# Routed experts after attention: the first two expert tiles share their split weights, VectorE subtracts for all tiles

## The chip, the cores and the metric

One core of a Trainium2 chip runs the whole program in one launch. The metric is the device time of one execution in microseconds (us), lower is better. The engines are called as in the profile: PE (TensorE matmul), PEld (its weight loads), DVE (VectorE), ACT (ScalarE), POOL (GpSimd), SP (SyncE, which issues most transfers).

## What is computed

```python
def reference(**kwargs):
    attn_out = _attn_ref(**attn_kwargs)          # sigmoid attention, 4 x 12 heads x 448 x 64
    x = np.ascontiguousarray(attn_out.transpose(0, 2, 1, 3)).reshape(B * S, H * D)
    x = _moe_ref(x=x, **moe_kwargs)              # 8 experts, one per token
    return _moe2_ref(x=x, **moe2_kwargs)         # sigmoid(x @ w_gate) * (x @ w_val) @ w_out

def _moe_ref(x, expert_emb, tau, w1, w2):        # x 1792 x 768, w1 8 x 768 x 1024, w2 8 x 1024 x 768
    ...
    expert_idx = np.argmax(logits, axis=1)
    ...
    for e in range(E):
        mask = expert_idx == e
        h = np.maximum(x[mask] @ w1[e], 0.0)
        out[mask] = gate_w[mask, None] * (h @ w2[e])
```

Everything is float32. The kernel keeps nearly that precision by writing each float32 operand as a high and a low part in the type fp32r and adding three products: high times high, low times high, high times low.

## The kernel before

The program runs three parts in a row. **Attention** works through 24 pairs of heads. **The experts** follow: tokens are sorted by expert into tiles of 128 rows; `NSTAT` = 14 tiles are written out in the program, further ones sit behind run-time branches (`tail_tiles`, L1074). **The feed-forward part** comes last.

For an expert tile p, `gather` (L791) fetches its 128 rows of x by an indirect transfer that POOL issues; `front` (L798) turns them by PE transposes, and ACT and DVE write the parts xh and xl; `h_chunk` (L923) multiplies by w1 in four chunks c of 9 matmuls; ACT applies relu; `turn` (L949) turns h and writes its parts (hh, hl, for tile 0 w64, w32); `y_chunk` (L965) multiplies by w2 in four chunks of 12 matmuls; `y_scale` and `y_out` weight the rows and scatter them.

Weights come as chunks of 128 x 1536. The list `order` (L128) names the chunks in the sequence in which they are used, `load` (L162) issues a chunk's transfer into one of eight raw buffers, `split_next` (L216) makes the next chunk's parts, and `take` hands them to the product. A split is a cast on ACT (hi) and a subtraction lo = raw - hi (L213), on DVE or, where `split_next` is given `G`, on POOL. The parts live in a ring of `RING` = 4 buffers: a cast for a chunk waits until the product of the chunk four places earlier is done.

Tiles 0 and 1 belong to the same expert, the fullest one, so that tile 1 needs no transfer; its w1 chunks are split a second time from the same raw buffers (`order` lists w1 for p = 0 and p = 1).

Between attention and tile 2 stands the routing: some 90 small DVE steps on tables of 128 x 8 to 128 x 208. `place_a` (L587) counts tiles per expert, `place_b` (L633) makes the table of experts, `place_c` (L673) the rows' places `am`; POOL multiplies them by row numbers (spi, L559), PE sums (psid, `ids_all`, L684), and DVE casts the sums into idx, the row numbers that `gather` of tiles 2 and on needs. `gate_a` to `gate_d` (L727 to L759) make the rows' weights: a root on POOL, a normalisation on DVE, an exponential on ACT, three multiplications on POOL (spg, L559), sums on PE (psg), and gate_s, which `y_scale` needs. PE's stream holds psid and psg between products, so it stands still if they are late.

No scheduler decides the order: the program's text, with `manual_schedule`, is the order on each engine, and each engine runs its own instructions strictly in that order. The four PSUM buffers (`slot`) are shared by all products.

```python
    G0 = 2 * NPR * (B - 1) + 2
    for g in range(2 * NP + 1):                                  # L834, attention
        ...
        if g == 2 * NP:
            split_next(eng=G, hi_eng=V)                          # L847, w1 chunk 3
    ...
    h_chunk(0, 0, lambda: count(TE, NT))                         # L1175
    ...
    for c in range(NW1):                                         # L1206, tile 1
        h_chunk(1, c)
        split_next(ahead, V if c in (0, 3) else G)
```

Of the kernel before, what the change touches and what calls it, by code (L numbers as in the profile page):

```python
# [105 lines left out]
def routed_kernel(ctx: ExitStack, tc: tile.TileContext, kqP, vP, emb, tau, w1P, w2P, wffP, cst, out):  # L106
# [21 lines left out]
    order = [("w1", p, c) for p in range(2) for c in range(NW1)] + [("w2", 0, c) for c in range(NW2)]  # L128
# [33 lines left out]
    def load(i):  # L162
        it, r = order[i], raws[raw_of[i]]
        if it[0] in ("w1", "w2"):
            w, (_, p, c) = {"w1": w1P, "w2": w2P}[it[0]], it

            if p != 1:
                e = expert_of(p)
                src = w[bass.ds(e, 1), :, c * CH : (c + 1) * CH].rearrange("a p f -> p (a f)")
                SP.dma_start(r, src, cond=(e != expert_of(p - 1)) if p else None)  # L170
# [38 lines left out]
    def split(raw, pool, name, width=CH, eng=V, hi_eng=None):  # L209
        hi = pool.tile([P, width], F32R, tag="hi", name=f"hi{name}")[:, : raw.shape[1]]  # L210
        lo = pool.tile([P, width], F32R, tag="lo", name=f"lo{name}")[:, : raw.shape[1]]
        (hi_eng.tensor_copy if hi_eng else A.copy)(hi, raw)  # L212
        eng.tensor_sub(lo, raw, hi)  # L213
        return hi, lo

    def split_next(ahead=None, eng=V, hi_eng=None):  # L216
# [4 lines left out]
        parts[i] = split(raws[raw_of[i]], ring, i, eng=eng, hi_eng=hi_eng)  # L221
# [610 lines left out]

    G0 = 2 * NPR * (B - 1) + 2
    for g in range(2 * NP + 1):  # L834
# [11 lines left out]
        if g == 2 * NP:  # L846
            split_next(eng=G, hi_eng=V)  # L847
# [63 lines left out]
        if q in (6, 7, 8):  # L911
            split_next(hi_eng=V if q == 7 else None)
# [10 lines left out]
    def h_chunk(p, c, between=None):  # L923
# [4 lines left out]
        hi, lo = take()  # L928
# [246 lines left out]
    h_chunk(0, 0, lambda: count(TE, NT))  # L1175
# [8 lines left out]
    h_chunk(0, 1, lambda: first_ids(1, NT))  # L1184
# [8 lines left out]
    place_a()  # L1193
    for k in range(2, NW2):
        load(order.index(("w2", 0, k)))
    ahead = []
    split_next(ahead)
    split_next(ahead, G)
    h_chunk(0, 2)
    split_next(ahead, G)  # L1200
    h_chunk(0, 3)
    front(1)
    turn(0, dp, ("w64", "w32"))
    gate_a()
    split_next(ahead)
    for c in range(NW1):  # L1206
        h_chunk(1, c)
        split_next(ahead, V if c in (0, 3) else G)
        if c == 0:
            place_b()  # L1210
    for i in ahead:
        load(i)

    part = [take() for _ in range(NW2)]
    y_chunk(0, 0, part[0])
    turn(1)
    place_c()
    gate_b()
    gate_exp()
    for c in range(1, NW2):  # L1220
        y_chunk(0, c, part[c])
    for c in range(NW2):
        y_chunk(1, c, part[c])
        if c == 0:
            ids_all()
            gather(2)
            gate_c()
            gather(3)
        if c == 2:
# [8 lines left out]
    for p in range(2, NSTAT):  # L1238
# [5 lines left out]
        for c in range(NW1):  # L1244
# [7 lines left out]
            split_next(None, G if p == 2 and c in (1, 3) else V)  # L1252
# [159 lines left out]
```

## Time and profile before

| | before |
|---|---|
| median of 3 runs | 1037.21 us (1036.66 to 1038.28) |
| profiled execution | 1037.45 us, span 1035.6 us |
| PE busy, share of the span | 1006.4 us, 97% |
| DVE busy | 597.2 us, 58% |
| ACT busy | 503.1 us, 49% |
| POOL busy | 138.4 us, 13% |

A row of the timeline gives the start of an instruction in us from the span's start, its duration, engine, line, operation, outputs and inputs with their shapes, how many equal ones are merged (x), and in brackets how long the engine was idle before it and what ended that. Such a duration includes time in which an instruction that has begun is held up. The view of waits sums the idle time by who ended it. A window gives, for a stretch of time, each engine's busy time and the clock that TensorE was granted as a share of full speed (1.00 is 2.4 GHz, 0.50 is 1.2 GHz).

### The profile page before, as it was taken

The numbers are of one execution on the slowest core, as the hardware profiler recorded it, in microseconds if no ns is written. First come the engines' busy times: TensorE is split into PE (matmuls) and PEld (weight loads), VectorE is DVE, ScalarE is ACT, GpSimd is POOL, SyncE is SP. The second block draws the span as 40 slices with busy tenths as digits, with TensorE's granted clock in tenths as the row PEclk, the third lists the DMA queues.
The fourth block names the chain that finished last, engine by engine and source line by source line (L and its number), as shares of the span: only waits on it lengthen the run. The fifth ranks groups of instructions, "written<-read, shape, count | busy, mean of one in ns | idle before, by whom it ended". The sixth has DMA issues, their size and how long they took to land.

```text
span 1035.6 us, 15304 instructions
## 1 busy us (share of the span) xinstructions
PE 1006.4 (97%) x6144; PEld 822.7 (79%) x6144; DVE 597.2 (58%) x660; ACT 503.1 (49%) x546; POOL 138.4 (13%) x109
## 2 busy tenths in 40 slices
PE   9999999878999999999999999999999999999996
PEld 4455455676887788888888899888899888899995
DVE  5665577986887877787658743334332333323551
ACT  5576678536766676777502432233322333323540
POOL 0010012643242122111100000200000000001001
PEclk9999999989999999999999999999999999999998
DMA  7878786112689876765458652422333333324630
GB/s 254 303 257 300 247 304 231 71 32 110 247 265 415 289 263 269 253 221 211 166 169 280 236 180 99 143 99 92 122 122 123 125 108 103 122 92 143 196 119 31
DMA packets 38526, 191.94 MB, mean 185 GB/s; under 512 B 4952, under 2 KB 5992, under 8 KB 36016
## 3 DMA queue, kind: packets, MB, share of 16 engines
q1 hardware_dynamic: 30560, 152.84, 43.3%
q0 software_dynamic: 7888, 38.05, 9.8%
q8 instruction: 50, 0.82, 0.3%
q14 instruction: 28, 0.23, 0.1%
HBM read 197.46 MB, written 31.16 MB: 221 GB/s over the span
## 4 chain that ended last, share of the span: by engine, by line
PE 73%; DVE 0%; issue 0%; DMA 0%; POOLq 0%; ACT 0%
PE gv L1154 11%; PE gv L1153 11%; PE gv L1155 11%; PE h L935 8%; PE o L921 5%; PE o L919 5%; PE o L920 5%; PE y L919 3%; PE y L921 3%; PE y L920 3%; PE qh L1024 1%; PE qy L1047 1%; PE hTp L954 1%; PE yTp L1139 1%; PE xTp L803 1%
## 5 line engine op out<-in xcount | busy, mean ns | idle before, releaser
L213 DVE TENSOR_TENSOR lo<-rawb,hi 128x1536 fp32r<-128x1536 f32 x173 | 302.1, 1756 | 289.9 <-ACT hi L212 286.3
L212 ACT CAST hi<-rawb 128x1536 fp32r<-128x1536 f32 x178 | 262.8, 1480 | 244.7 <-PE gv L1154 96.3
L1153 PE MATMUL gv<-yT,hi 128*128 128x512 f32 (+1 forms) x576 | 208.9, 363 | 0.0
L1155 PE MATMUL gv<-yT,lo 128*128 128x512 f32 (+1 forms) x576 | 208.9, 363 | 0.0
L1154 PE MATMUL gv<-yT,hi 128*128 128x512 f32 (+1 forms) x576 | 208.8, 363 | 0.0
L1155 PEld LDWEIGHTS gv<-yT,lo 128*128 128x128 f32 x576 | 108.7, 189 | 16.9
L1153 PEld LDWEIGHTS gv<-yT,hi 128*128 128x128 f32 x576 | 108.7, 189 | 16.8
L1154 PEld LDWEIGHTS gv<-yT,hi 128*128 128x128 f32 x576 | 108.7, 189 | 16.7
L919 PE MATMUL o<-hi,gh 128*128 128x384 f32 x336 | 112.8, 336 | 0.0
L921 PE MATMUL o<-lo,gh 128*128 128x384 f32 x336 | 112.3, 334 | 0.0
L920 PE MATMUL o<-hi,gl 128*128 128x384 f32 x336 | 112.3, 334 | 0.0
L359 ACT ACTIVATE attn<-sc,bias_s 112x896 f32<-112x896 f32 x96 | 91.2, 1001 | 41.9 <-PE sc L358 41.9
L1324 ACT CAST gh<-sg 128x512 fp32r<-128x512 f32 (+1 forms) x48 | 27.2, 567 | 132.1 <-DVE sg L1323 132.1
L364 PE MATMUL av<-attn,v 112*64 112x448 f32 x384 | 82.8, 552 | 0.0
L919 PE MATMUL y<-hi,hh 128*128 128x384 f32 x208 | 72.7, 349 | 0.0
L935 PE MATMUL h<-hi,xh 128*128 128x512 f32 x168 | 69.2, 412 | 3.5 <-PEq L1078 3.4
L935 PE MATMUL h<-lo,xh 128*128 128x512 f32 x168 | 67.1, 399 | 4.5 <-DVE lo L213 4.5
L921 PE MATMUL y<-lo,hh 128*128 128x384 f32 x208 | 70.5, 339 | 0.3 <-DVE lo L213 0.3
L920 PE MATMUL y<-hi,hl 128*128 128x384 f32 x208 | 70.3, 338 | 0.0
L1343 POOL DMA_INDIRECT out<-ob,idc x13 | 17.8, 1373 | 370.5 <-DVE ob L1372 340.1
L920 PEld LDWEIGHTS o<-hi,gl 128*128 128x128 f32 x336 | 63.1, 188 | 0.1
L919 PEld LDWEIGHTS o<-hi,gh 128*128 128x128 f32 x336 | 63.1, 188 | 0.1
(302 smaller groups left out, 1311.9 us busy)
## 6 DMA issues: line engine op xcount, KB each, us to landing
rawb<-wd SPq DMA_DIRECT2D x65, 768.0 KB
rawb<-in_w1P SPq DMA_DIRECT2D x52, 768.0 KB
rawb<-in_w2P SPq DMA_DIRECT2D x52, 768.0 KB
rawb<-in_wffP SPq DMA_DIRECT2D x16, 1536.0 KB
wd<-rawb POOLq DMA_DIRECT2D x16, 768.0 KB, 7.9
kq<-in_kqP SPq DMA_DIRECT2D x24, 448.0 KB
v<-in_vP SPq DMA_DIRECT2D x24, 224.0 KB
xd<-xr_sb POOLq DMA_DIRECT2D x12, 336.0 KB, 5.2
```

What stands on the lines that cost most here:

```text
L212: (hi_eng.tensor_copy if hi_eng else A.copy)(hi, raw)
L213: eng.tensor_sub(lo, raw, hi)
L359: A.activation(at_, ps[:CP, :, :S], AF.Sigmoid, bias=bias_s[:CP], scale=1.0 / math.sqrt(HD))
L364: T.matmul(pav_t[i][j * HD : (j + 1) * HD, 0, :S], v[:, c, j * HD : (j + 1) * HD], attn_t[i, c][:, j, :], start=(c == 0), stop=(c == NCH - 1))
L919: T.matmul(o, ah[:, ks], bh[:, w], start=(k == 0), stop=False)
L920: T.matmul(o, al[:, ks], bh[:, w], start=False, stop=False)
L921: T.matmul(o, ah[:, ks], bl[:, w], start=False, stop=(k == nk - 1))
L935: T.matmul(ps[:, half, :], x[:, k * P : (k + 1) * P], w[:, s * 512 : (s + 1) * 512], start=(k == 0 and x is xh and w is hi), stop=(k == KD ...
L1153: T.matmul(o, hi[:, a, k, :], yh[:, k, :n], start=(k == 0), stop=False)
L1154: T.matmul(o, hi[:, a, k, :], yl[:, k, :n], start=False, stop=False)
L1155: T.matmul(o, lo[:, a, k, :], yh[:, k, :n], start=False, stop=(k == KD - 1))
L1324: A.copy(gh[:, f, :n], sg[:, :n])
```

## The change

- `order` lists w1 for tile 0 alone. `h_chunk` takes a chunk's parts as an argument, and `w1_0` holds the four chunks' parts until tile 1 has used them too. Four splits go: of twelve for tiles 0 and 1 there remain eight.
- `split` and `split_next` lose their engine argument: DVE does every subtraction. The cast of w1 chunk 3, which DVE made at the end of attention (L847), is made by ACT behind `first_ids` of tile 1.
- The steps between tile 0's w1 product and tile 2 stand in another order: `place_a` and `gate_a` behind tile 0's w1 product, then `front(1)`, `place_b`, the transfers `ahead`, `place_c`, and only then `turn(0)`, tile 1's w1 product with the splits of w2, `ids_all` and the gathers of tiles 2 and 3, before tile 0's first w2 chunk; `gate_b`, `gate_exp` before `turn(1)`; `gate_c` before tile 1's w2 product; `front(2)`, `gate_d` and `y_scale(0)` behind its second chunk, not its third.

```diff
--- before.py
+++ after.py
@@ -125,7 +125,8 @@
 
     rawb = rawp.tile([P, RAWS, CH], F32, name="rawb")
     raws = [rawb[:, i, :] for i in range(RAWS)]
-    order = [("w1", p, c) for p in range(2) for c in range(NW1)] + [("w2", 0, c) for c in range(NW2)]
+
+    order = [("w1", 0, c) for c in range(NW1)] + [("w2", 0, c) for c in range(NW2)]
     order += [("w1", 2, c) for c in range(NW1)]
     for p in range(3, NSTAT):
         order += [("w1", p, c) for c in range(NW1)]
@@ -163,11 +164,9 @@
         it, r = order[i], raws[raw_of[i]]
         if it[0] in ("w1", "w2"):
             w, (_, p, c) = {"w1": w1P, "w2": w2P}[it[0]], it
-
-            if p != 1:
-                e = expert_of(p)
-                src = w[bass.ds(e, 1), :, c * CH : (c + 1) * CH].rearrange("a p f -> p (a f)")
-                SP.dma_start(r, src, cond=(e != expert_of(p - 1)) if p else None)
+            e = expert_of(p)
+            src = w[bass.ds(e, 1), :, c * CH : (c + 1) * CH].rearrange("a p f -> p (a f)")
+            SP.dma_start(r, src, cond=(e != expert_of(p - 1)) if p else None)
         elif it[0] == "gv":
             if it[1] == 0 and it[2] in direct:
                 if it[2] - 2 not in direct:
@@ -206,19 +205,19 @@
     parts = {}
     done_split = [0]
 
-    def split(raw, pool, name, width=CH, eng=V, hi_eng=None):
+    def split(raw, pool, name, width=CH, hi_eng=None):
         hi = pool.tile([P, width], F32R, tag="hi", name=f"hi{name}")[:, : raw.shape[1]]
         lo = pool.tile([P, width], F32R, tag="lo", name=f"lo{name}")[:, : raw.shape[1]]
         (hi_eng.tensor_copy if hi_eng else A.copy)(hi, raw)
-        eng.tensor_sub(lo, raw, hi)
+        V.tensor_sub(lo, raw, hi)
         return hi, lo
 
-    def split_next(ahead=None, eng=V, hi_eng=None):
+    def split_next(ahead=None, hi_eng=None):
         i = done_split[0]
         if i >= len(order):
             return
         done_split[0] += 1
-        parts[i] = split(raws[raw_of[i]], ring, i, eng=eng, hi_eng=hi_eng)
+        parts[i] = split(raws[raw_of[i]], ring, i, hi_eng=hi_eng)
         j = next((j for j in range(i + 1, len(order)) if order[j][:2] == ("gv", 0) and order[j][2] in direct), None)
         if j == i + 1:
             f = order[j][2]
@@ -830,6 +829,8 @@
         split_pair(n)
         load_pair(n + 3)
 
+    ahead = []
+
     G0 = 2 * NPR * (B - 1) + 2
     for g in range(2 * NP + 1):
         i, hh = divmod(g, 2)
@@ -843,8 +844,6 @@
         elif g == 4:
             prepare_experts()
         q = g - G0
-        if g == 2 * NP:
-            split_next(eng=G, hi_eng=V)
         ia, ha = divmod(g - 1, 2)
         if q == 2:
             count(0, TE)
@@ -909,7 +908,7 @@
             for k in (0, 1):
                 load(order.index(("w2", 0, k)))
         if q in (6, 7, 8):
-            split_next(hi_eng=V if q == 7 else None)
+            split_next(ahead, hi_eng=V if q == 7 else None)
 
     hp_t = {}
 
@@ -920,12 +919,12 @@
         T.matmul(o, al[:, ks], bh[:, w], start=False, stop=False)
         T.matmul(o, ah[:, ks], bl[:, w], start=False, stop=(k == nk - 1))
 
-    def h_chunk(p, c, between=None):
+    def h_chunk(p, c, between=None, part=None):
         if c == 0:
             hp_t[p] = slot(f"h{p}")
         ps = hp_t[p]
         xh, xl = xg_t["T", p]
-        hi, lo = take()
+        hi, lo = part or take()
 
         passes = ((xh, hi), (xh, lo), (xl, hi))
         for part in (passes[:2], passes[2:]) if c == 0 else (passes,):
@@ -1172,7 +1171,8 @@
     A.copy(x.rearrange("p (b c) n -> p b c n", c=2), pv[:, :, :, :P])
     SP.dma_start(xd[TE * CP :, D - P :].rearrange("(c p) n -> p c n", p=CP), x)
     choose(TE, NT)
-    h_chunk(0, 0, lambda: count(TE, NT))
+    w1_0 = [take() for _ in range(NW1 - 1)]
+    h_chunk(0, 0, lambda: count(TE, NT), part=w1_0[0])
     fullest_ids(TE, NT)
     for f in squares:
         f()
@@ -1181,7 +1181,7 @@
     ranks(TE, NT)
     first_tiles(TE, NT, (1,))
     columns(TE, NT)
-    h_chunk(0, 1, lambda: first_ids(1, NT))
+    h_chunk(0, 1, lambda: first_ids(1, NT), part=w1_0[1])
     at.close()
     yTp = ctx.enter_context(tc.tile_pool(name="yT", bufs=1, reuse_waits="tile"))
     ytp = ctx.enter_context(tc.tile_pool(name="yt", bufs=2, reuse_waits="tile"))
@@ -1190,43 +1190,38 @@
     decp = ExitStack()
     dp = decp.enter_context(tc.tile_pool(name="dec", bufs=1, side="right", reuse_waits="tile"))
     gather(1)
-    place_a()
     for k in range(2, NW2):
         load(order.index(("w2", 0, k)))
-    ahead = []
     split_next(ahead)
-    split_next(ahead, G)
-    h_chunk(0, 2)
-    split_next(ahead, G)
-    h_chunk(0, 3)
+    w1_0.append(take())
+    h_chunk(0, 2, part=w1_0[2])
+    h_chunk(0, 3, part=w1_0[3])
+    place_a()
+    gate_a()
     front(1)
-    turn(0, dp, ("w64", "w32"))
-    gate_a()
-    split_next(ahead)
-    for c in range(NW1):
-        h_chunk(1, c)
-        split_next(ahead, V if c in (0, 3) else G)
-        if c == 0:
-            place_b()
+    place_b()
     for i in ahead:
         load(i)
+    place_c()
+    turn(0, dp, ("w64", "w32"))
+    for c in range(NW1):
+        h_chunk(1, c, part=w1_0[c])
+        split_next()
+    ids_all()
+    gather(2)
+    gather(3)
 
     part = [take() for _ in range(NW2)]
     y_chunk(0, 0, part[0])
-    turn(1)
-    place_c()
     gate_b()
     gate_exp()
+    turn(1)
     for c in range(1, NW2):
         y_chunk(0, c, part[c])
+    gate_c()
     for c in range(NW2):
         y_chunk(1, c, part[c])
-        if c == 0:
-            ids_all()
-            gather(2)
-            gate_c()
-            gather(3)
-        if c == 2:
+        if c == 1:
             front(2)
             gate_d()
             y_scale(0)
@@ -1249,7 +1244,7 @@
                 turn(2)
                 small_ids()
                 gather_small()
-            split_next(None, G if p == 2 and c in (1, 3) else V)
+            split_next()
             if c == 1 and p - PZ in (0, 1, 3):
                 small_step((0, 2, 0, 6)[p - PZ])
             if dec and c % 2 == 0:
```

The line numbers of the changed kernel are one to five lower. In the names below, the number behind lo, hi is the chunk's place in `order`: before, 0 to 3 are w1 for tile 0, 4 to 7 for tile 1, 8 to 11 w2 of both, 12 to 19 w1 of tiles 2 and 3; in the change, 0 to 3 are w1 of both tiles, 4 to 7 w2, 8 to 15 w1 of tiles 2 and 3.

POOL, from the end of attention to the gather of tile 4. Before:

```order
L213 TENSOR_TENSOR lo3_1995<-rawb_91,hi3_1994 128x1536
L794 DMA xg1_2126<-xd_71,idx01_139 128x768
L213 TENSOR_TENSOR lo5_2170<-rawb_91,hi5_2169 128x1536
L213 TENSOR_TENSOR lo6_2183<-rawb_91,hi6_2182 128x1536
L730 TENSOR_TENSOR root_158<-ss_118,half_s_109 112x16
L213 TENSOR_TENSOR lo9_2289<-rawb_91,hi9_2288 128x1536
L213 TENSOR_TENSOR lo10_2302<-rawb_91,hi10_2301 128x1536
L559 TENSOR_TENSOR spi_2371<-am_151,ids_h_113 112x416
L794 DMA xg2_2450<-xd_71,idx_133 128x768
L559 TENSOR_TENSOR spg_2462<-am_151,g3_2456 112x16x26 x3
L794 DMA xg3_2466<-xd_71,idx_133 128x768
L794 DMA xg4_2569<-xd_71,idx_133 128x768
```

In the change:

```order
L793 DMA xg1_2122<-xd_71,idx01_139 128x768
L729 TENSOR_TENSOR root_158<-ss_118,half_s_109 112x16
L558 TENSOR_TENSOR spi_2257<-am_151,ids_h_113 112x416
L793 DMA xg2_2350<-xd_71,idx_133 128x768
L793 DMA xg3_2352<-xd_71,idx_133 128x768
L558 TENSOR_TENSOR spg_2435<-am_151,g3_2429 112x16x26 x3
L793 DMA xg4_2553<-xd_71,idx_133 128x768
```

The five subtractions are gone from POOL, as are two more behind the gather of tile 4 (lo17, lo19); the root, spi and spg remain in the same order, and the gather of tile 3 stands ahead of spg.

DVE, the end of `place_a` (offs is its last result) up to the first step of `place_b` (end). Before:

```order
L619 TENSOR_TENSOR offs_145<-offs_145,nz_2152 128x8
L213 TENSOR_TENSOR lo4_2166<-rawb_91,hi4_2165 128x1536
L809 TENSOR_TENSOR xl1_2206<-xTp1_2198,xh1_2205 128x768
L960 TENSOR_TENSOR w320_2219<-hTp0_2209,w640_2218 128x1024
L729 TENSOR_REDUCE ss_118<-ssp_119 112x4
L731 TENSOR_TENSOR sh_159<-lg_117,mx_120 112x128
L213 TENSOR_TENSOR lo7_2226<-rawb_91,hi7_2225 128x1536
L213 TENSOR_TENSOR lo8_2240<-rawb_91,hi8_2239 128x1536
L636 TENSOR_TENSOR end_2243<-offs_145,st_144 128x8
```

In the change:

```order
L618 TENSOR_TENSOR offs_145<-offs_145,nz_2175 128x8
L728 TENSOR_REDUCE ss_118<-ssp_119 112x4
L730 TENSOR_TENSOR sh_159<-lg_117,mx_120 112x128
L808 TENSOR_TENSOR xl1_2197<-xTp1_2189,xh1_2196 128x768
L635 TENSOR_TENSOR end_2200<-offs_145,st_144 128x8
```

Four subtractions, of weights and of h, that stood between `place_a` and `place_b` are gone from there or stand later.

DVE, from the last step of `place_c` (am) to the first of `gate_b` (root). Before, with the two subtractions ahead of `place_c`:

```order
L670 CAST et_2277<-ef_2274 1x26
L213 TENSOR_TENSOR lo11_2317<-rawb_91,hi11_2316 128x1536
L960 TENSOR_TENSOR hl1_2360<-hTp1_2350,hh1_2359 128x1024
L675 CAST ky_2363<-tn_156 128x26
L676 TENSOR_TENSOR s3_131<-oh_123,cs_92 112x128
L678 TENSOR_REDUCE po_2366<-s3_131 112x16
L680 TENSOR_TENSOR ab_2368<-ai_140,po_2366 112x16
L681 TENSOR_TENSOR am_151<-ky_2363,ab_2368 112x416
L299 TENSOR_SCALAR root_158<-root_158 112x16
```

In the change:

```order
L680 TENSOR_TENSOR am_151<-ky_2249,ab_2254 112x416
L959 TENSOR_TENSOR w320_2269<-hTp0_2259,w640_2268 128x1024
L212 TENSOR_TENSOR lo4_2283<-rawb_91,hi4_2282 128x1536
L212 TENSOR_TENSOR lo5_2297<-rawb_91,hi5_2296 128x1536
L212 TENSOR_TENSOR lo6_2311<-rawb_91,hi6_2310 128x1536
L212 TENSOR_TENSOR lo7_2327<-rawb_91,hi7_2326 128x1536
L685 CAST idx_133<-psid_2331 128x26
L686 COPY idf_154<-psid_2331 32x5
L298 TENSOR_SCALAR root_158<-root_158 112x16
```

Tile 0's h (w32) and the four w2 subtractions now stand in one row behind `place_c`, and idx ahead of the normalisation. The subtraction hl of tile 1 stands seven rows further down, behind the normalisation.

## Rows read from the trace of the kernel before

**Rows 1.** Waits of PE, whole span (engine line waited for: us in total, times, longest us).
```profile
PE y L921 <- DVE lo L213: 4.0, 2, 3.7
```

**Rows 2.** Two windows of 10 us: busy of PE, PEld, DVE, ACT, POOL, granted clock, DMA.
```profile
230.00:240.00 10.00, 10.00 (x52) 8.85 (x50) 5.91 (x7) 7.37 (x6) 1.92 (x3) 0.87 0.41 116
...
240.00:250.00 10.00, 6.55 (x26) 4.98 (x25) 7.07 (x7) 4.47 (x4) 6.62 (x2) 0.83 0.31 126
```

**Rows 3.** Timeline of POOL, 185 to 230 us (start us, us, engine line op, names, shapes).
```profile
185.01 6.88 POOL L213 TENSOR_TENSOR lo<-rawb,hi 128x1536 fp32r<-128x1536 f32 x2 [1.59 <-ACT hi L212]
...
196.94 4.60 POOL L730 TENSOR_TENSOR root<-ss,half_s 112x16 f32<-112x16 f32 x1 [5.05 <-DVE ss L729]
...
202.23 6.96 POOL L213 TENSOR_TENSOR lo<-rawb,hi 128x1536 fp32r<-128x1536 f32 x2 [0.68 <-ACT hi L212]
...
225.43 3.99 POOL L559 TENSOR_TENSOR spg<-am,g 112x416 f16<-112x416 f16 x1
```

**Rows 4.** Timeline of DVE: the long steps, and one of usual length.
```profile
185.17 3.35 DVE L610 TENSOR_TENSOR st<-st,qz 128x8 f32<-128x8 f32 x1
...
188.56 3.37 DVE L613 COPY ns<-st 128x8 f32<-128x8 f32 x1
...
192.10 0.17 DVE L616 TENSOR_TENSOR ns<-tot,nz 128x8 f32<-128x8 f32 x1
...
202.38 3.40 DVE L647 TENSOR_TENSOR isa<-cs,nq 128x26 f32<-128x26 f32 x1
...
205.70 3.54 DVE L648 TENSOR_TENSOR jbv<-cs,nq 128x26 f32<-128x26 f32 x1
```

**Rows 5.** Timeline of ACT, 180 to 221 us.
```profile
180.91 1.46 ACT L212 CAST hi<-rawb 128x1536 fp32r<-128x1536 f32 x1
...
189.01 0.81 ACT L808 CAST xh<-xTp 128x768 fp32r<-128x768 f32 x1 [0.40 <-PE xTp L803]
...
207.66 1.02 ACT L959 CAST hh<-hTp 128x1024 fp32r<-128x1024 f32 x1 [0.50 <-PE hTp L954]
...
220.47 0.31 ACT L738 ACTIVATE sh<-sh 112x128 f32<-112x128 f32 x1 [10.49 <-DVE sh L735]
```

**Rows 6.** Timeline of DVE: where each routing step begins.
```profile
182.03 0.15 DVE L589 COPY tot<-pk 128x8 f32<-128x8 f32 x1
...
193.05 1.75 DVE L213 TENSOR_TENSOR lo<-rawb,hi 128x1536 fp32r<-128x1536 f32 x1
...
201.67 0.16 DVE L636 TENSOR_TENSOR end<-offs,st 128x8 f32<-128x8 f32 x1
...
214.08 1.76 DVE L213 TENSOR_TENSOR lo<-rawb,hi 128x1536 fp32r<-128x1536 f32 x1
...
216.89 0.17 DVE L675 CAST ky<-tn 128x26 f16<-128x26 f32 x1
...
218.32 0.17 DVE L299 TENSOR_SCALAR root<-root 112x16 f32<-112x16 f32 x1
...
222.01 0.26 DVE L742 TENSOR_REDUCE gs<-sh 112x16 f32<-112x128 f32 x1
...
225.27 3.41 DVE L213 TENSOR_TENSOR lo<-rawb,hi 128x1536 fp32r<-128x1536 f32 x2
```

**Rows 7.** Chain that ended last, one whole h product of a later tile.
```profile
292.19 8.20 PE h L935 x36
```

**Rows 8.** Timeline of PE, 194 to 234 us.
```profile
194.85 0.60 PE L935 MATMUL h<-lo,xh 128*128 128x512 f32 x1 [4.49 <-DVE lo L213]
...
204.50 0.34 PE L919 MATMUL y<-hi,w 128*128 128x384 f32 x1
...
206.59 1.03 PE L954 MATMUL hTp<-cs,hr 128*128 128x128 f32 x8
...
229.47 1.20 PE L566 MATMUL psg<-spg,bm 112*128 112x78 f16 x16 [2.35 <-POOL spg L559]
...
233.66 0.39 PE L935 MATMUL h<-hi,xh 128*128 128x512 f32 x1
```

## The prediction

> **What bounds the kernel now.** The page of the profile comes first: PE is busy for 97% of the span, DVE for 58%, POOL for 13%. Elsewhere PE is the limit, and only what PE loses can be won. PE's timeline and the view of its waits say where. Before 194.85 PE stood still for 4.49 us, in tile 1's w1 product, for a DVE subtraction lo [rows 8]. The w2 products waited 4.0 us for such a lo, in two waits of which the longer took 3.7 us [rows 1]. Before psg, at 229.47, PE waited 2.35 us for POOL's spg [rows 8]. All this is the stretch that the change rewrites. After such waits the granted clock of a 10 us window is below 1 (0.87 and 0.83 [rows 2]): half clock for a while, so that each wait costs more than itself.
>
> Why is DVE late there? In its timeline, four table steps of 128 x 8 or 128 x 26 take 3.35, 3.37, 3.40 and 3.54 us; one of the same 128 x 8 shape takes 0.17 [rows 4]. POOL's timeline explains it. POOL runs two subtractions back to back from 185.01 for 6.88 us, to 191.89; the two long steps begin at 185.17 and 188.56, and the second ends at 191.93. Again POOL from 202.23 for 6.96 us, to 209.19, and the other two long steps fill 202.38 to 209.24 [rows 3, 4]. While POOL subtracts, DVE gets one small step through per subtraction. So a subtraction given to POOL does not relieve DVE: it takes about 3.4 us of DVE's time, where DVE's own takes 1.75 [rows 6].
>
> The Trainium skill states the mechanism (SBUF — State Buffer, Who interferes with whom): a DVE instruction with two SBUF inputs, or in a two-port mode, and a GpSimd instruction that reads SBUF exclude each other for a whole instruction, whichever began first. The trace agrees, with the four steps above. Another page speaks against the change (Perfetto Trace Analysis, Optimizing Scalar/DVE Operations): where DVE is saturated, moving work off it to GpSimd may pay, though it warns that the two share a port. By that rule alone, DVE, which in the new order is busy almost without a break from 191 to 208 us, would only become later; by the rows it gets 3.4 us back for each 1.75 us taken over. The sum below uses the rows alone.
>
> **The change, part by part.** I follow the new order on the old trace's clock. Durations are differences of starts.
>
> *DVE.* ACT casts w1 chunk 3 at 180.91 and is done at 182.4 [rows 5], before PE needs that chunk. The subtraction takes 1.75: 184.1. `place_a` took 182.03 to 193.05, 11.02 us, of which the two long steps are 6.72; at 0.17 each it takes 4.6: 188.8. `gate_a` has two steps: 189.1. xl1 waits for xh1, which ACT ends at 189.82 [rows 5], then takes some 1.0: 190.8. `place_b` took 201.67 to 214.08, 12.4 us, with 6.94 in long steps, hence 5.8: 196.6. `place_c` 216.89 to 218.32, 1.4: 198.1. Tile 0's h: one subtraction of weights and one of h took 214.08 to 216.89, so the latter 1.1: 199.2. The four w2 subtractions at 1.7 (two take 3.41): 206.0. The casts of idx, 0.2, and the normalisation, 218.32 to the exponential at 220.47, 2.15: 208.4. Then ACT's exponential 0.31 and its cast of tile 1's h 1.02 with two handovers: 209.8; hl 1.1 to 1.2: 211.0. `gate_c`, 222.01 to 225.27, 3.3: 214.2 [all rows 6, 5].
>
> *POOL.* The root took 4.60 us; it can start at 189 and is wanted at 206. spi follows `place_c`. spg's third part took 3.99 us in the old order, because two DVE subtractions began just ahead of it at 225.27 and held it up for 3.41 us [rows 3, 6]: it ended 0.74 us after them, which I take as what it needs. Now at most one subtraction can go ahead of it (lo8, whose cast waits for tile 1's first w2 chunk). spg is ready at 215.0, or at 216.8 if lo8 wins.
>
> *PE.* xh1 is there at 189.8, the parts of w1 are those of tile 0, xl1 comes at 190.8 while six matmuls run: no wait. The product takes 8.2 us [rows 7]: 198.1, where it used to end at 204.50 [rows 8]. This is the first stall with its slow stretch. Then psid waits about 1 us for spi, and tile 0's w2 product for lo4 at 199.2 + 1.7 = 200.9; psid's small matmuls lie inside that. A w2 chunk takes 2.09 us (204.50 to 206.59 [rows 8]). Ten of the first twelve matmuls, the turn of tile 1 (1.0) and three chunks: 209.9; lo5 to lo7 are always there in time. Tile 1's second matmul waits for hl, 211.0; two chunks: 215.0; front(2), six transposes against the turn's eight in 1.03 us, 0.8: 215.8; psg at 215.8 or 216.8, 0.6 (1.20 at half clock [rows 8]); two chunks: tile 2 begins at 220.6 to 221.6. Before it began at 233.66 [rows 8]. **Gain 12.1 to 13.1 us.** Behind that, ACT waits for gate_s before it casts w1 chunks 1 to 3 of tile 2: lo8 and xl2 end at 218, gate_s at 219, ACT's scaling (0.9) and cast (1.46) at 221.4, lo9 at 223.1; its use stands at 222.9, so 0.2 us is lost.
>
> *Tile 2.* Two subtractions come back from POOL, 3.5 us more for DVE. They are hidden: in the two windows concerned DVE was busy 5.91 and 7.07 of 10 us, and part of the 7.07 is again a step held up by POOL [rows 2]. Without that cover they would cost their 3.5. Since DVE's steps behind them come slightly sooner relative to PE, the small second wait of [rows 1], 4.0 less 3.7 = 0.3 us, should go.
>
> *Transfers.* Tile 1 loads nothing before or after. The table of experts is ready at 196.6 instead of 214.1, so SP issues the loads of tile 2 earlier; no wait of PE for a weight transfer stands here now. The new gathers read x as before. Four dropped splits take 6 us from ACT or DVE beside the path and otherwise cost nothing.
>
> *The sum.* -13.1 for tile 2's start, or -12.1; +0.2 and -0.3 behind it: about -13.0 against the profiled execution's 1037.45, so 1024.4. The median of the runs is 0.24 lower, and I give **1024.3 us**.
>
> **Ends of what the trace does not show.** Whether new waits of about 1 us each, twice near 199 us and once near 211, bring the half clock: with none, 0; with a slow stretch at 201, the loss of some 1.7 us is hidden up to 1.1 by the wait for hl. I take none, because the falls I see stand behind waits of 2.35 us and more. The other way, the half clock behind the branch to the tail tiles (in the window with 0.83 [rows 2]) might not come, up to -1.7.
>
> **Rivals.**
>
> 1. *The root holds the chain.* POOL's root now runs beside the two-input steps of `place_b`. If it and they exclude each other, either DVE stands still until 193.7, 2.9 us late, or the root runs only behind `place_c`, 198.1 + 4.6 = 202.7, and spi, psid and all of PE's products come 3 to 4 us late. Time 1027.5 to 1028.5. For it: the four long steps. Against it: the root ran 196.94 to 201.54 [rows 3], and the DVE subtraction of 1.75 us that stands just ahead of `place_b` was over when that began at 201.67 [rows 6], so it ran while the root ran. 0.20.
>
> 2. *Only the first stall goes.* PE ends tile 1's w1 product 6.4 us earlier, but the chain of DVE, now one piece from 182 to 214 us, loses half of the 13 us again (ACT's cast of h behind the exponential, handovers from engine to engine). Tile 2 then starts 6.5 us earlier: time about 1031. 0.08.
>
> 3. *Slower.* The four long steps are long in themselves, and POOL's timing beside them is chance. Then the chain keeps 6.72 + 6.94 - 4 x 0.17 = 13.0 us, tile 2 starts at 233.6 to 234.6, and the two subtractions of tile 2 are no longer covered, +3.5. Time 1038 to 1042. It decides if these steps stay at 3.4 us. Against it: the step of the same shape at 0.17, and two ends that agree with POOL's to 0.05 us. 0.03. Between it and rival 2 lies no change, 0.02: PE waits as long for psg and hl as it now does for lo.
>
> 4. *The change doesn't do what it says*, if a ring buffer with shared parts were overwritten or awaited early. Each w2 cast waits for the chunk four places back, now used by tile 1, so the casts come at 192, 194, 196 and 199 us, all before DVE reaches them at 199.2. It changes nothing in the sum.
>
> **How the numbers follow.** A measurement of this kernel tells about 0.2%, 2.1 us, from no change. My forecast, 1022.5 to 1026, has 0.67; rival 1 0.20, rival 2 0.08, no change 0.02, rival 3 0.03. For 8 in 10 the range takes in rival 1 with 0.5 above it, and below the forecast the missing half clock and 0.6 for the rounding of some fifteen durations: 1022.0 to 1029.0. Faster 0.95, same 0.02, slower 0.03.
>
> **What would show it.** In the new profile the four steps take below 0.4 us and POOL has no subtraction; tile 1's w1 product runs as one block from 190 to 198 us; PE's waits for lo are about 1 us; psg comes near 216 us, tile 2 near 221. Wrong if one of the four steps is still above 1 us, if DVE waits for POOL's root, if PE's wait before psg stays at 2 us, or if a later wait of PE gives back what is won.

## The result and the profile after

| | after | before, same series |
|---|---|---|
| median | 1023.82 us (4 runs, 1022.70 to 1025.91) | 1037.01 us (4 runs) |
| ratio, 95% interval | 0.9876 (0.9860 to 0.9891) | |
| profiled execution | 1024.48 us, span 1022.6 us | 1037.45 us, span 1035.6 us |

The change makes the kernel 13 us, 1.2%, faster; the forecast was 1024.3 us. The page's busy times of the changed kernel:

```profile
PE 1003.8 (98%) x6144; PEld 821.3 (80%) x6144; DVE 584.5 (57%) x662; ACT 498.1 (49%) x543; POOL 104.5 (10%) x102
```

POOL has 33.9 us less to do, and although DVE took over five of its seven subtractions (the other two fell away with the sharing) DVE has 12.7 us less too: four splits are gone, and so is the time in which DVE's steps were held up. PE's waits between 180 and 300 us (engine, line, waited for: us in total, times, longest; PEq is PE's sequencer, here at the branch to the tail tiles):

```profile
PE h L934 <- PEq L1077: 4.1, 1, 4.1
PE xTp L802 <- DMA xg<-xd,idx: 1.5, 2, 1.0
PE y L920 <- DVE lo L212: 0.8, 1, 0.8
PE psid L565 <- POOL spi L558: 0.7, 1, 0.7
```

The 4.0 us for lo [rows 1] are 0.8 us; the 4.49 us in tile 1's w1 product are gone, and psg has no wait at all [rows 8]. The longest wait left is that at the branch to the tail tiles. DVE's timeline shows where the change came from:

```profile
182.76 1.76 DVE L212 TENSOR_TENSOR lo<-rawb,hi 128x1536 fp32r<-128x1536 f32 x1 [0.77 <-ACT hi L211]
...
187.46 0.17 DVE L609 TENSOR_TENSOR st<-st,qz 128x8 f32<-128x8 f32 x1
187.66 0.17 DVE L612 COPY ns<-st 128x8 f32<-128x8 f32 x1
...
191.69 0.16 DVE L646 TENSOR_TENSOR isa<-cs,nq 128x26 f32<-128x26 f32 x1
191.78 0.17 DVE L647 TENSOR_TENSOR jbv<-cs,nq 128x26 f32<-128x26 f32 x1
...
199.34 6.75 DVE L212 TENSOR_TENSOR lo<-rawb,hi 128x1536 fp32r<-128x1536 f32 x4
...
209.13 1.23 DVE L959 TENSOR_TENSOR hl<-hTp,hh 128x1024 fp32r<-128x1024 f32 x1 [1.28 <-ACT hh L958]
```

The second to fifth of these rows are the four long steps of [rows 4], the same instructions on the same shapes: 0.16 to 0.17 us where they took 3.35 to 3.54. POOL's timeline has no subtraction left:

```profile
189.20 2.95 POOL L729 TENSOR_TENSOR root<-ss,half_s 112x16 f32<-112x16 f32 x1 [5.93 <-DVE ss L728]
198.37 0.89 POOL L558 TENSOR_TENSOR spi<-am,ids_h 112x416 f16<-112x416 f16 x1 [6.22 <-DVE am L680]
...
211.56 2.86 POOL L558 TENSOR_TENSOR spg<-am,g 112x416 f16<-112x416 f16 x3 [2.74 <-DVE g L746]
```

All three parts of spg together now take 2.86 us; the third alone took 3.99 [rows 3]. PE's timeline, from tile 1's w1 product to tile 3's first matmul:

```profile
190.12 0.50 PE L934 MATMUL h<-hi,xh 128*128 128x512 f32 x1
...
199.31 0.55 PE L565 MATMUL psid<-spi,bm 112*128 112x26 f16 x16 [0.73 <-POOL spi L558]
...
201.14 0.48 PE L920 MATMUL y<-lo,w 128*128 128x384 f32 x1 [0.83 <-DVE lo L212]
...
204.30 1.29 PE L953 MATMUL hTp<-cs,hr 128*128 128x128 f32 x8
...
211.69 0.34 PE L918 MATMUL y<-hi,hh 128*128 128x384 f32 x1
...
216.51 0.76 PE L565 MATMUL psg<-spg,bm 112*128 112x78 f16 x16
...
221.34 0.40 PE L934 MATMUL h<-hi,xh 128*128 128x512 f32 x1
...
234.44 0.47 PE L934 MATMUL h<-hi,xh 128*128 128x512 f32 x1 [4.06 <-PEq L1077]
```

Tile 2 starts at 221.34 instead of 233.66 [rows 8], 12.3 us earlier. Tile 3 starts at 234.44 instead of 246.17, 11.7 earlier: 0.6 goes back at the branch, where the wait is 4.06 us and was 3.45. By 270 us the lead is 12.9 us, and it stays there to the end (13.0). Nearly everything was won in one stretch, and the rest of the program only carries it.

### The profile page after: what moved, and what is told of

Same layout as the page of the kernel before. It is cut to its first block, busy times and chain, and to the rows that moved or that the text cites. A ratio compares the mean times of both kernels' runs of the same rounds, so it can differ in the third digit from the quotient of the medians.

```text
span 1022.6 us, 15298 instructions
## 1 busy us (share of the span) xinstructions
PE 1003.8 (98%) x6144; PEld 821.3 (80%) x6144; DVE 584.5 (57%) x662; ACT 498.1 (49%) x543; POOL 104.5 (10%) x102
## 4 chain that ended last, share of the span: by engine, by line
PE 93%; DMA 3%; issue 1%; DVE 1%; ACT 0%; POOLq 0%; another core or an unknown queue 0%; DVEq 0%
PE gv L1154 11%; PE gv L1153 11%; PE gv L1152 11%; PE h L934 9%; PE av L363 8%; PE sc L357 6%; PE o L920 6%; PE o L919 5%; PE o L918 5%; PE y L918 4%; PE y L920 4%; PE y L919 4%; PE qh L1023 2%; DMA xg<-xd,idx 1%; PE qy L1046 1%
## 5 line engine op out<-in xcount | busy, mean ns | idle before, releaser
L212 DVE TENSOR_TENSOR lo<-rawb,hi 128x1536 fp32r<-128x1536 f32 x176 | 307.1, 1757 | 292.3 <-ACT hi L211 287.7
L211 ACT CAST hi<-rawb 128x1536 fp32r<-128x1536 f32 x175 | 258.1, 1480 | 240.0 <-PE gv L1153 96.3
L920 PEld LDWEIGHTS o<-lo,gh 128*128 128x128 f32 x336 | 63.1, 188 | 0.0
```

What stands on the lines that cost most here:

```text
L212: V.tensor_sub(lo, raw, hi)
L920: T.matmul(o, ah[:, ks], bl[:, w], start=False, stop=(k == nk - 1))
```

## The experiments

Three theories stood beside each other. Mine: while POOL subtracts, DVE is held for about 3.4 us. The rivals: the steps are long in themselves, so POOL relieves DVE; or the order of the steps alone brought the gain. Ratios are to the kernel before on the same chip (the changed kernel: 0.9876).

**1. Only the engine: the old order, nothing shared, all subtractions on DVE.**

```diff
-        eng.tensor_sub(lo, raw, hi)
+        V.tensor_sub(lo, raw, hi)
```

> The kernel before, with nothing changed but the engine of the eight POOL subtractions: VectorE does them all. No split is shared and the order of the steps is the old one. Theory (a POOL subtraction holds DVE for about 3.4 us, DVE's own takes 1.75): the four long steps fall to below 0.4 us, DVE gets back some 3.2 us per pair of subtractions, two pairs stand on the path, so tile 2 starts 3 to 6.5 us earlier: 1031 to 1034 us. Rival A (the four steps are long in themselves, POOL relieves DVE): they stay at 3.4 us, DVE has 1.75 us more for each, 1040 us or more. Rival B (all that helped is the sharing and the order): within 1 us of the kernel before.

Measured: 1029.55 us, ratio 0.9933 (0.9916 to 0.9951), so 6.3 us lower and more than I had expected. Giving DVE the seven subtractions of POOL (the expectation counts one too many) made the kernel faster: both rivals fall. Tile 2 starts at 226.14, 7.5 us earlier. The four long steps of [rows 4] in this run, on DVE's timeline:

```profile
185.73 0.17 DVE L610 TENSOR_TENSOR st<-st,qz 128x8 f32<-128x8 f32 x1
185.94 0.17 DVE L613 COPY ns<-st 128x8 f32<-128x8 f32 x1
...
198.61 0.17 DVE L647 TENSOR_TENSOR isa<-cs,nq 128x26 f32<-128x26 f32 x1
198.70 0.17 DVE L648 TENSOR_TENSOR jbv<-cs,nq 128x26 f32<-128x26 f32 x1
```

DVE now holds POOL instead; POOL's timeline, then DVE's:

```profile
194.48 6.29 POOL L730 TENSOR_TENSOR root<-ss,half_s 112x16 f32<-112x16 f32 x1 [10.49 <-DVE ss L729]
```

```profile
194.51 3.42 DVE L213 TENSOR_TENSOR lo<-rawb,hi 128x1536 fp32r<-128x1536 f32 x2
```

The root of 2.95 us takes 6.29, that is 3.34 more, about the length of the two DVE subtractions that began 0.03 us after it.

**2. Only the sharing: the old order, POOL keeps what is left to it.**

```diff
-    order = [("w1", p, c) for p in range(2) for c in range(NW1)] + [("w2", 0, c) for c in range(NW2)]
+    order = [("w1", 0, c) for c in range(NW1)] + [("w2", 0, c) for c in range(NW2)]
...
-    split_next(ahead)
-    split_next(ahead, G)
-    h_chunk(0, 2)
-    split_next(ahead, G)
-    h_chunk(0, 3)
+    h_chunk(0, 2, part=w1_0[2])
+    h_chunk(0, 3, part=w1_0[3])
...
-        h_chunk(1, c)
+        h_chunk(1, c, part=w1_0[c])
         split_next(ahead, V if c in (0, 3) else G)
```

> The kernel before with the shared parts alone: tile 1 takes tile 0's split w1, its own four splits are gone; the order of the steps is the old one, and the subtractions that remain on POOL (the last of tile 0's w1, two of w2, two of tile 2) stay there. Theory: the two long steps of the first table go, since their subtractions are gone, and two subtractions of 1.75 us leave DVE; the two long steps of the second table stay at 3.4 us; PE's 4.49 us wait goes. Tile 2 starts 6 to 10 us earlier: 1027 to 1031 us. Rival A (long in themselves): all four long steps stay, 1033 to 1036 us. Rival B (the order alone brought the gain): 1035 to 1037 us.

Measured: 1030.30 us, ratio 0.9945 (0.9929 to 0.9962), within the theory's range; but tile 2 starts at 229.51 in the profile (the slowest of the four executions), 4.2 us earlier, where I had expected 6 to 10. The two steps of the first table take 0.17 us, and PE's wait of 4.49 us is gone. POOL's subtractions for w2 remain, and with them the two long steps of the second table. POOL's timeline, then DVE's:

```profile
197.76 6.99 POOL L213 TENSOR_TENSOR lo<-rawb,hi 128x1536 fp32r<-128x1536 f32 x2 [0.59 <-ACT hi L212]
```

```profile
198.07 3.27 DVE L647 TENSOR_TENSOR isa<-cs,nq 128x26 f32<-128x26 f32 x1
201.26 3.54 DVE L648 TENSOR_TENSOR jbv<-cs,nq 128x26 f32<-128x26 f32 x1
```

They moved to 198 us together with the subtractions and still end with them. The long steps follow POOL, not their own line.

**3. Sharing and engine, in the old order.** The two edits above together.

> The kernel before with shared parts and all subtractions on VectorE, in the old order of the steps: all of the change but its order. Theory: no long step is left, 1.6 us per POOL subtraction are won against the run with shared parts alone: 1024.5 to 1028 us, that is most of the gain; the order is worth what is left, 1 to 4 us. Rival B (the order alone brought the gain): 1033 us or more. Rival A (long in themselves): 1033 us or more, with four steps at 3.4 us.

Measured: 1026.64 us, ratio 0.9914 (0.9897 to 0.9930), inside the expected range. The two parts are worth 6.3 and 5.5 us alone and 9.2 together, less than their sum: two of the subtractions that hold DVE are among those that sharing drops. The order, with the later split of w1 chunk 3 and its cast on ACT, adds the rest, some 2.4 to 3.9 us (0.9914 to 0.9891 in run 11, whose interval overlaps this one, or to 0.9876, whose interval does not). Of these two waits of PE in run 3 it removes the first, and shortens the second to 0.8 us:

```profile
PE psg L566 <- POOL spg L559: 2.4, 1, 2.4
PE y L922 <- DVE lo L213: 1.4, 1, 1.4
```

The wait for spg is the same lock turned round: spg's three parts, from 214.26, take 5.97 us here, with two DVE subtractions from 216.08 beside the third, and 2.86 us in the changed kernel, where none stands there. So part of what the order brings is the lock too.

**4. The changed kernel with two of the w2 subtractions back on POOL.**

```diff
-        split_next()
+        split_next(eng=G if c in (1, 2) else V)
```

> The changed kernel with two of tile 0's four w2 subtractions (chunks 1 and 2) back on POOL. Theory: each blocks DVE's two-input steps for about 3.4 us where DVE's own took 1.7; the chain to the subtraction hl of tile 1 gets about 3.3 us longer, 210.36 to 213.7, and tile 2 starts 2 to 3.3 us later: 1025.8 to 1027.2 us, a step of above 3 us stands again in DVE's timeline. Rival (POOL relieves DVE): the chain gets 3.4 us shorter, PE alone bounds the stretch, and the time falls by 0 to 1.5 us: 1022.3 to 1023.8 us.

Measured: 1032.98 us, ratio 0.9971 (0.9956 to 0.9986): 9 to 10 us slower than the changed kernel. The direction is the theory's, the size three times what I expected. POOL's, DVE's and PE's timelines:

```profile
198.93 6.81 POOL L212 TENSOR_TENSOR lo<-rawb,hi 128x1536 fp32r<-128x1536 f32 x2
```

```profile
199.06 9.97 DVE L212 TENSOR_TENSOR lo<-rawb,hi 128x1536 fp32r<-128x1536 f32 x2
```

```profile
207.41 0.69 PE L920 MATMUL y<-lo,w 128*128 128x384 f32 x1 [7.38 <-DVE lo L212]
```

The DVE row holds two subtractions, of 8.30 and 1.75 us by the list of this tile's instructions (ns, shortest, median, longest):

```profile
L212 DVE TENSOR_TENSOR lo<-rawb,hi x2: 1746/5022/8299, 199.1 to 207.3; 128x1536 fp32r<-128x1536 f32 x2
```

The first is lo4, which PE needs before the two that POOL makes. It began 0.13 us behind POOL's first and got no turn between the two, so all 6.81 us stand ahead of it. I had charged a delay at the end of DVE's chain; it hit the first product.

**5 and 6. The lock by itself.** One POOL instruction is added behind the root, beside `place_b`; its result is unused. In 5 it is a subtraction (the last line but one), in 6 a memset (the last line).

```diff
     gate_a()
+    junk = yTp.tile([P, KD, 512], F32R, tag="yT0", name="junk")
+    junk = junk.rearrange("p k n -> p (k n)")
+    G.tensor_sub(junk[:, :CH], raws[raw_of[3]], w1_0[3][0])
+    G.memset(junk.bitcast(F32), 0.0)
```

> The changed kernel with one POOL subtraction added, of the same shape as those removed (128 x 1536, two operands in SBUF), behind the root; its result is not used by anything, so nothing waits for it but what the chip imposes. Theory: it runs beside place_b for about 3.4 us, one or two steps of place_b take some 3.3 us instead of 0.2 to 0.4, everything behind them on DVE comes 3 us later, tile 2 starts 2 to 3.3 us later: 1025.8 to 1027.2 us. Rival (steps long in themselves, or POOL harmless): no step above 0.5 us, 1023.3 to 1024.3 us.

> The changed kernel with one POOL memset added in the place of that extra subtraction (128 x 3072, it writes SBUF and reads nothing there); its result is not used. Theory (what blocks is an instruction of POOL with operands read from SBUF beside a DVE instruction with two inputs there): no step of place_b is longer than 0.5 us, 1023.3 to 1024.3 us. Rival (any work of POOL on SBUF blocks DVE): one step of place_b as long as the memset, and the time up by about that length less 1 us.

Measured: with the subtraction 1030.72 us, ratio 0.9937 (0.9917 to 0.9956), 6 to 7 us slower than the changed kernel; with the memset 1024.17 us, ratio 0.9875 (0.9852 to 0.9897), the same as the changed kernel. POOL's timeline, then DVE's, with the subtraction:

```profile
188.83 2.95 POOL L729 TENSOR_TENSOR root<-ss,half_s 112x16 f32<-112x16 f32 x1 [5.92 <-DVE ss L728]
191.77 3.51 POOL L1203 TENSOR_TENSOR junk<-rawb,hi 128x1536 fp32r<-128x1536 f32 x1
```

```profile
190.68 4.62 DVE L635 TENSOR_TENSOR end<-offs,st 128x8 f32<-128x8 f32 x1
```

The same two with the memset:

```profile
191.87 2.66 POOL L1203 MEMSET junk<- 128x3072 f32 x1
```

```profile
190.75 0.16 DVE L635 TENSOR_TENSOR end<-offs,st 128x8 f32<-128x8 f32 x1
...
191.98 0.19 DVE L649 SCALAR_TENSOR_TENSOR jbv<-isa,jbv 128x26 f32<-128x26 f32 x1
```

One POOL subtraction that nothing waits for costs DVE 4.62 us in one step of 8 columns, which ends with POOL's instruction (195.30 and 195.28). A memset of 2.66 us in the same place holds up nothing. So it isn't POOL's being busy that counts. The Trainium skill says so too (SBUF — State Buffer, Who interferes with whom): DVE instructions with two SBUF inputs contend with GpSimd instructions that read SBUF, not with those that only write it. These two runs agree. The root does not: it reads SBUF and held none of DVE's steps (last section). My size was again too small: PE waited 5.2 us before psid, and in the window from 205 to 210 us the granted clock was 0.50.

**7. Tile 2's two subtractions back on POOL.**

```diff
-            split_next()
+            split_next(eng=G if p == 2 and c in (1, 3) else V)
```

> The changed kernel with two of tile 2's w2 subtractions (chunks 1 and 3 of those made during its w1 product) back on POOL, as before the change. Theory: they stand where DVE has time to spare, so that place is worth little: 0 to 0.8 us slower, 1023.8 to 1024.6 us, by a short wait of PE for a lo in the tile behind, as the kernel before had. Rival (POOL relieves DVE): 0 to 0.5 us faster.

Measured: 1024.50 us, ratio 0.9883 (0.9865 to 0.9900), not to be told from the changed kernel. The lock is there all the same (POOL, then DVE), with nothing behind it that is late:

```profile
231.42 3.72 POOL L212 TENSOR_TENSOR lo<-rawb,hi 128x1536 fp32r<-128x1536 f32 x1 [1.20 <-ACT hi L211]
```

```profile
231.76 3.42 DVE L703 SCALAR_TENSOR_TENSOR tn<-ef,tn 128x26 f32<-128x26 f32 x1
```

**8. The order taken further.**

```diff
-    def place_b():
+    def place_b(between):
...
+        between()
         STT(out=jb, in0=jb, scalar=0.0, in1=isa, op0=ALU.max, op1=ALU.subtract)
...
     front(1)
-    place_b()
...
-    place_c()
     turn(0, dp, ("w64", "w32"))
-    for c in range(NW1):
-        h_chunk(1, c, part=w1_0[c])
-        split_next()
-    ids_all()
...
+    h_chunk(1, 0, part=w1_0[0])
+    place_b(lambda: split_next(ahead))
...
+    h_chunk(1, 1, part=w1_0[1])
+    split_next()
+    place_c()
...
     y_chunk(0, 0, part[0])
+    turn(1)
+    y_chunk(0, 1, part[1])
+    ids_all()
...
     gate_b()
     gate_exp()
-    turn(1)
...
         if c == 1:
             front(2)
-            gate_d()
-            y_scale(0)
+        if c == 3:
+            gate_d()
         split_next()
+    y_scale(0)
     y_scale(1)
```

> The changed kernel with the order taken further: tile 0's h is turned and subtracted ahead of place_b; the first w2 subtraction stands in the middle of place_b and the second ahead of place_c; tile 1's turn comes right behind tile 0's first w2 chunk, and its subtraction hl ahead of the normalisation; the ids' product behind the second chunk; the gates' product behind all of tile 1's w2 chunks. Theory (after the change DVE's chain to hl and two waits of 0.7 and 0.8 us with the half clock behind them set tile 2's start): PE has no wait from 190 to 217 us, no half clock near 201 us, tile 2 starts at 218.2 instead of 221.3: 1020.3 to 1021.5 us. Rival (the chain of DVE sets the end in any order, through spg and gate_s): 1023 to 1024.5 us.

Measured: 1024.62 us, ratio 0.9886 (0.9866 to 0.9905): no gain. By the time it looks like the rival; the rows say otherwise. POOL's, DVE's and PE's timelines:

```profile
202.92 4.00 POOL L558 TENSOR_TENSOR spi<-am,ids_h 112x416 f16<-112x416 f16 x1 [11.07 <-DVE am L681]
```

```profile
202.76 3.42 DVE L212 TENSOR_TENSOR lo<-rawb,hi 128x1536 fp32r<-128x1536 f32 x2
```

```profile
206.97 0.58 PE L565 MATMUL psid<-spi,bm 112*128 112x26 f16 x16 [3.47 <-POOL spi L558]
```

spi takes 4.00 us where it took 0.89 in the changed kernel, because two DVE subtractions began 0.16 us ahead of it. In the changed kernel tile 0's subtraction of h stands there, which reads one of its inputs from PSUM; it too began 0.16 us ahead of spi (198.21), and spi ran beside it undisturbed. The same lock, the other way round.

**9. The same, with spi on DVE; 10. the same, with spi on POOL and its product later.**

```diff
-        gp["i"] = spread(am, [ids_h], "i")
+        gp["i"] = spread(am, [ids_h], "i", V)
```

```diff
-    ids_all()
...
     for c in (2, 3):
         y_chunk(0, c, part[c])
+    ids_all()
...
-        if c == 1:
+        if c == 2:
             front(2)
```

> The order taken further, as before, but spi (112 x 416, float16, one instruction) is made on VectorE instead of POOL. Theory (in that run spi on POOL took 4.00 us instead of 0.89, because two DVE subtractions had begun 0.16 us ahead of it, and PE stood 3.47 us before psid; the same lock, the other way round): on DVE it takes 0.3 to 0.6 us right behind place_c, PE's wait before psid falls to below 0.5 us, the half clock behind it goes, tile 2 starts at 218 to 219.5 us: 1020 to 1022 us. Rival (the chain of DVE sets the end in any order): tile 2 not before 221 us, 1023 us or more.

> The order taken further, spi on POOL as in the changed kernel, but its product psid behind all of tile 0's w2 chunks, and the turn of tile 2's rows behind the third of tile 1's w2 chunks instead of the second. Theory: spi still takes 4 us on POOL, ending near 207, but PE reaches psid only near 208 and does not wait; tile 2 starts at 218 to 219.5 us if its rows are gathered by 214.5: 1020 to 1022 us. Rival: the gather, which now starts near 208.6, is late (tile 1's took 6.1 us from its issue to PE's use), PE waits 1 to 2 us for it and gives back most: 1022 to 1023.5 us.

Measured: 1021.69 us, ratio 0.9861 (0.9841 to 0.9880), and 1022.01 us (five runs, 1020.22 to 1025.52), ratio 0.9862 (0.9840 to 0.9884). PE's timeline of run 9:

```profile
203.47 0.56 PE L565 MATMUL psid<-spi,bm 112*128 112x26 f16 x16
...
205.14 0.44 PE L921 MATMUL y<-lo,w 128*128 128x384 f32 x1 [0.66 <-DVE lo L212]
...
218.05 0.77 PE L565 MATMUL psg<-spg,bm 112*128 112x78 f16 x16
218.65 0.48 PE L935 MATMUL h<-hi,xh 128*128 128x512 f32 x1
```

psid has no wait, and tile 2 starts at 218.65, as expected. That is 2.7 us before the first profile of the changed kernel, which has a half clock near 201 us, and 1.1 before that of run 11, which has none. In run 10 spi again takes 4.00 us, but PE comes later and does not wait for it; tile 2 starts at 219.71. Its time lies on the border between the two forecasts. The rival's late gather is not there: what PE waits for is spg, 0.58 us, whose three parts take 5.97 us beside two DVE subtractions from 214.93.

**11 and 12. The changed kernel and run 9's on one chip.**

> The changed kernel itself, on one chip with the run that follows, so that the two can be compared. Theory: ratio to the kernel before 0.986 to 0.989 as before; the half clock near 201 us comes in some executions and not in others, since PE's two waits of some 0.8 us ahead of it are the only ones there.

> The order taken further with spi on VectorE, again, beside the changed kernel on the same chip. Theory: tile 2 starts 1 to 3 us earlier than in the changed kernel, and nothing behind it gives that back: median 1 to 3 us lower than that of the run ahead of this one. Rival: the earlier result was the scatter of the measurement; the two medians lie within 0.5 us.

Measured: 1024.44 us, ratio 0.9891 (0.9871 to 0.9911), against 1022.18 us, ratio 0.9856 (0.9835 to 0.9878): 2.3 us apart, the theory's side (run 11's own ratio is just above the expected 0.989). The two intervals overlap by 0.0007, but all four times of run 12 (1019.75 to 1023.10) lie below all four of run 11 (1023.54 to 1026.81). In the profiles tile 2 starts at 218.47 against 219.73, and the whole span is 1.3 us shorter. So this version beats the kernel before, and by this one pair of runs the changed kernel by 1.3 (profiles) to 2.3 us (medians). The profile of run 11 also shows the changed kernel without the half clock near 201 us. Its PE timeline, to be read beside that of the first profile:

```profile
200.87 0.44 PE L920 MATMUL y<-lo,w 128*128 128x384 f32 x1 [0.84 <-DVE lo L212]
...
202.72 1.03 PE L953 MATMUL hTp<-cs,hr 128*128 128x128 f32 x8
...
219.73 0.40 PE L934 MATMUL h<-hi,xh 128*128 128x512 f32 x1
...
233.36 0.47 PE L934 MATMUL h<-hi,xh 128*128 128x512 f32 x1 [4.60 <-PEq L1077]
```

And the window from 202 to 204 us, of the first profile and of run 11 (the PEclk column, third from the end, is 0.50 and 1.00):

```profile
202.00:204.00 2.00, 2.00 (x8) 2.00 (x8) 2.00 (x2) 0.36 (x1) 0.00 (x0) 0.50 0.00 0
```

```profile
202.00:204.00 2.00, 2.00 (x17) 1.96 (x16) 2.00 (x2) 0.09 (x1) 0.00 (x0) 1.00 0.00 0
```

The waits ahead are the same to 0.01 us in both. The ten matmuls up to hTp, the turn of tile 1's h, take 3.16 us in one and 1.85 in the other. Tile 2 starts 1.6 us earlier without the half clock, but 0.27 of that was there before the two waits: from the first of the ten matmuls to tile 2 it is 20.20 us against 18.86, so the half clock costs 1.3 (20.19 against 18.86 in runs 6 and 7). Tile 3 starts only 1.1 us earlier, since the wait at the branch grows from 4.06 to 4.60.

## Why the prediction was right, step by step

- **The long steps are POOL's doing.** Right, and shown: they go when the engine alone changes (1), they move with POOL's subtractions (2), they come back with one unused subtraction (5) and not with a memset (6). The place to see it beforehand was that their ends agreed with POOL's.
- **DVE's chain.** Forecast and measured: first subtraction done 184.1 and 184.5, `place_a` and `gate_a` 189.1 and 189.3, xl1 190.8 and 191.0, `place_b` 196.6 and 196.8, tile 0's h 199.2 and 199.4, four w2 subtractions 206.0 and 206.0. The largest miss is hl, 211.0 forecast and 210.4 measured, as the normalisation took 1.7 us and not 2.15. The old 2.15 contained one more held step, which I had overlooked: L301 took 0.59 us beside spi, and takes 0.17 now (L300).
- **PE.** Tile 1's w1 product ran without a wait, 190.12 to 198.4; forecast 189.9 to 198.1. psid waited 0.7 us, tile 0's product 0.8 us for lo; forecast about 1 each. psg came at 216.5, forecast 215.8 to 216.8, and without a wait: spg was ready at 214.4. lo8, which I feared ahead of spg's third part, came only at 215.35.
- **The gain to tile 2.** 12.3 us, within 12.1 to 13.1. It contains a loss that I had taken as none: "I take none, because the falls I see stand behind waits of 2.35 us and more." The half clock did come, behind two waits of 0.73 and 0.83 us, in the first profile and in run 6's, but not in those of runs 7 and 11, which are the same up to there. It cost 1.6 us up to tile 1's first w2 matmul, near the 1.7 of the bound; but only 0.2 of it was hidden by hl, where I had allowed up to 1.1, because without it PE reaches hl only 0.1 us before it is ready. So this term was wrong as a yes or no: it is something that an execution has or has not. Without it (run 11) tile 2 starts 13.9 us earlier, more than I forecast, mostly because hl came sooner; that the first profile lies inside 12.1 to 13.1 is partly luck.
- **Behind tile 2.** I forecast +0.2 and -0.3. The +0.2 did not come: lo9 was done at 223.3, and its use stood at 223.4. There was +0.6 at the branch to the tail tiles, which I had not costed, -0.5 in tile 2's w2 product, where the second small wait for lo is gone as forecast, and -0.65 before the sixth tile's front. That last wait (before: 1.09 us for ACT's hr) is there in run 6 as well, so the change can't be given credit for it. The sum came out at 13.0, as predicted, partly because these misses cancel. The sum itself was loose: its terms give -13.2 or -12.2, of which I took -13.0 without a reason, and 0.24 below 1024.45 is 1024.2, not 1024.3.
- **Tile 2's subtractions, costed at nothing.** Right: run 7.
- **The rivals.** The root (rival 1) did not hold the chain: 2.95 us from 189.20, with DVE's two-input steps from 190.98 on at 0.16 us. Its 4.60 us before had 1.65 us of a hold by a DVE subtraction in it, which I had not taken out. Only the first stall (rival 2) falls with the result: tile 2 starts 12.3 us earlier, not 6.5. Slower (rival 3) falls with run 1. Rival 4, the ring that may be awaited early, cost nothing: the four w2 subtractions run in one row from 199.34, without a wait for a cast.

## What to carry to other kernels

A small step that takes 3.4 us where its twin takes 0.17, and ends with another engine's instruction, is a wait that the profile counts as busy time; look for it before moving work to the engine that seems idle. An elementwise operation with two SBUF inputs is not moved off VectorE by giving it to GpSimd while VectorE runs such operations itself: here it cost DVE 3.4 us per instruction instead of 1.75. And the other way round, a short GpSimd instruction that PE waits for (spi, 0.89 us) wants a DVE neighbour that reads PSUM, or to be done on DVE: beside two subtractions it took 4.00.

## What was not expected of the hardware

- The held engine can lose more than one turn. In run 4 a DVE subtraction that began just behind the first of two POOL subtractions waited for both, 8.30 us; before the change one small step passed between two of them [rows 3, 4].
- In run 5 the held step began at 190.68, while POOL was still at its root (to 191.78) and 1.09 us before the recorded start of the subtraction. With the memset in that place the step of that line took 0.16 us, so it was not the root that held it. Whether POOL takes hold ahead of the start that the profile records was not tried.
- The root takes 2.95 us undisturbed, 4.60 with one DVE subtraction just behind its start [rows 3] and 6.29 with two (run 1): it is held by DVE, but its own run held none of DVE's two-input steps in the changed kernel. Nor did it meet the second DVE subtraction that ran beside it before the change (from 199.99, 1.76 us). So the lock does not last for the whole of this instruction; whether it lasts only for its beginning was not tried.
- A DVE step with a single input is held too. One of the four long steps, L613, is a copy of one input (3.37 us [rows 4]); and in the changed kernel two casts of one input (L749, 112 x 16) take 0.75 us beside spg, where the cast of the same shape just before them takes 0.18. No run isolates this.
- Behind two waits of PE of 0.73 and 0.83 us the granted clock fell to 0.50 in two profiles, and stayed at 1.00 in two others with the same waits. What decides it, no run shows.
